# A fused attention and two-layer kernel: q of chunks 1 to 3 scaled into tiles of their own and ahead of the scores, the state products reordered, the first loads in another order, two of three filler groups gone

## The chip, the cores and the metric

The kernel runs on one core of a Trainium2 chip. The metric is the device time of one execution in microseconds (us). Three runs of the kernel before took 582.59, 583.01 and 583.29 us, median 583.01.

## The reference

Linear attention with a decay per head, and then two dense layers with their own activations (B=2, H=8, S=768, D=64; 1536 tokens, d_model 512, d_ff 2048):

```
for t in range(S):                        # attention, state is 64x64 per batch and head
    state = gamma * state + outer(k[t], v[t])
    y[t]  = (1/sqrt(D)) * q[t] @ state
x = y as tokens x 512
h = x @ w_in;  g = max(h,0) + alpha*min(h,0);          x = g @ w_out      # layer 1
h = x @ w2_in; P = a0 + a1 h + a2 h^2 + a3 h^3
Q = 1 + |b0||h| + |b1| h^2;  g = P / (Q + 1e-6);       out = g @ w2_out   # layer 2
```

## The kernel before, in words

**Attention by chunks.** The tokens of the two batches are cut into 12 chunks of 128 (6 per batch). A chunk c has a scores part and an output part. `att_b(c)` (L132) is the scores part: 16 small matmuls (called sc, L139) of the transposed k tile `t` with the q tile, two DVE multiplications by the decay mask `dm_sb` that give `s` (L143), and for every chunk but a batch's first one the scaled q: four ACT multiplications by a constant per piece (L150) and one multiplication by `dq_sb` (L152, POOL for c < 4, DVE after that). For c < 6 the scaled q takes the place of q itself. `att_k(c)` (L114) scales the k tile in place: one POOL instruction (L123), or eight on ACT (L120) for chunks 4 to 7. `att_c(c)` (L154) is the output part: 16 matmuls of v with s into y (L170), 16 of k with v into the state's increment st (L182), 16 of the old state R with the scaled q, added to y (L193, the state product; not for a batch's first chunk), then the new state (L203 for a first chunk, else R = R + st on DVE, L205), and y split into a high part xh (ACT, L212) and a low part xl (DVE, L213). In the text sc1, y1, st1, ys1, xh1, xl1, R1 are these steps of chunk 1, qs1 its scaled q, k1 its scaled k; "b1" and "c1" are its two parts.

**The dense layers.** Weights arrive as 64-bit words and are decoded to a high and a low fp32r half: abs (ACT, L278), word (three DVE instructions, L284, L288, L292), hi (ACT, L303), lo (DVE, L309). `START` gives each half-matrix its half-step and `dec` the half-steps of its four decoding stages; `half(t)` issues what is due at t. A step h is 12 matmuls (`pe_h`, L334: for each of four k-pieces wh with xh, wh with xl, wl with xh); a step acc is 12 more (`pe_out`, L351). There are 96 of each.

**Order.** Every engine executes its instructions in the order in which the program issues them; the order is written out by hand. First come 8 warm-up matmuls and the first loads, all on SP's queue (L526 to L541), then the list `order` (L549): b0, c0, b1, b2, c1, b3, c2, c3, each followed by a `half`. Ahead of c0, b1 and b2 `keep_warm` puts 3, 2 and 3 fp32 filler matmuls on PE (L547; a trace counts two instructions for each). Then b4, and the main loop over the steps, which starts with the first h, c4, b5, the second h, and so on. Chunks 5 to 11 are placed in the main loop by `stages`. `alloc` hands out 42 SBUF slots in the order in which they came free; a load into a reused slot waits for its last user. `load_next(depth)` keeps up to depth raw weight tiles on their way.

Loads 1 to 28 of SP's queue before: q0, t0, dm, cst, k0, v0, q1, t1, w0, q2, t2, k1, v1, dq, q3, t3, k2, v2, k3, v3, w1, w2, alpha, pa, pb, q4, t4, k4 (q, t, k, v of a chunk and dq 256 KB each; dm and each raw weight tile w 512 KB; the others small).

Of the kernel before, what the change touches and what calls it, by code (L numbers as in the profile page):

```python
# [10 lines left out]
AF = mybir.ActivationFunctionType  # L11
# [3 lines left out]
P = 128  # L15
# [16 lines left out]
def tile_fused(  # L32
# [34 lines left out]
    def drop(t):  # L67
        free.append(slot.pop(id(t))[0])
# [19 lines left out]
    def xs(hl, b, ks, sl):  # L88
        return (xh, xl)[hl][b][:, ks, sl]
# [11 lines left out]
    def load_kq(c):  # L101
        nc.sync.dma_start(out=att[c]["q"], in_=qT[c])
        nc.sync.dma_start(out=att[c]["t"], in_=kT[c])  # L103

    def load_nv(c):
        nc.sync.dma_start(out=att[c]["k"], in_=kn[c])
        nc.sync.dma_start(out=att[c]["v"], in_=vn[c])

    def att_load(c):
        att_tiles(c)  # L110
# [15 lines left out]
    def rows(c, j):  # L126
        if c < CPB or j < 2:
            return [(slice(0, P), slice(0, P))]
        h = [slice(0, 64), slice(64, P)]
        return [(h[1], h[0]), (h[0], h[1])]  # L130

    def att_b(c, bank):  # L132
        a = att[c]
        ps = [bank(f"sc{c}_{e}") for e in range(2)]
        for j in range(NK):
            js = slice(j * P, (j + 1) * P)
            for e in range(2):
                es = slice(64 * e, 64 * e + 64)
                nc.tensor.matmul(ps[e][:, js], a["t"][es, js], a["q"][es, js], start=True, stop=True)  # L139
        a["s"] = alloc(f"s{c}")  # L140
        for e in range(2):
            es = slice(512 * e, 512 * e + 512)
            nc.vector.tensor_tensor(out=a["s"][:, es], in0=ps[e], in1=dm_sb[:, es], op=ALU.mult)  # L143
        if c % CPB > 0:
            a["qs"] = a["t"] if c > CPB else a["q"]
            for j in range(NK):
                js = slice(j * P, (j + 1) * P)
                o = 8 * CPB + 4 * (c % CPB) + j
                for ds, es in rows(c, j):
                    nc.scalar.mul(a["qs"][ds, js], a["q"][es, js], cst_sb[es, o:o + 1])  # L150
            eng = nc.gpsimd if c < 4 else nc.vector
            eng.tensor_tensor(out=a["qs"], in0=a["qs"], in1=dq_sb, op=ALU.mult)  # L152

    def att_c(c, ybank, pbank):  # L154
        a = att.pop(c)
        first = c % CPB == 0
        last = c % CPB == CPB - 1
        four = c >= CPB
        ys = [ybank(f"y{c}_{n}") for n in range(1 + four)]


        def yo(j, e):
            js = slice(P * (j % 2), P * (j % 2) + P) if four else slice(j * P, (j + 1) * P)
            return ys[j // 2 if four else 0][64 * e:64 * e + 64, js]

        heads = [(j, e) for j in ((0, 2, 1, 3) if four else range(NK)) for e in range(2)]
        starts = (0, 2) if four else (0,)
        for j, e in heads:
            h = 2 * j + e
            nc.tensor.matmul(  # L170
                yo(j, e),
                a["v"][:, 64 * h:64 * h + 64],
                a["s"][:, 512 * e + j * P:512 * e + (j + 1) * P],
                start=j in starts,
                stop=first and j == NK - 1,
            )
        if not last:
            pst = ys[0][:, 256:512] if four else pbank(f"st{c}")[:, 0:256]
            for j, g in heads:
                e = 1 - g if four and j >= 2 else g  # L180
                hs = slice(64 * (2 * j + e), 64 * (2 * j + e) + 64)
                nc.tensor.matmul(  # L182
                    pst[64 * g:64 * g + 64, 64 * j:64 * j + 64],
                    a["k"][:, hs],
                    a["v"][:, hs],
                    start=not four,
                    stop=not four or (first and j == NK - 1),
                )
        if not first:
            for j, e in heads:  # L190
                g = 1 - e if four and j >= 2 else e
                gs = slice(64 * g, 64 * g + 64)
                nc.tensor.matmul(  # L193
                    yo(j, e),
                    R[gs, j, :],
                    a["qs"][gs, j * P:(j + 1) * P],
                    start=False,
                    stop=j == NK - 1 or (four and j == 1),
                )
        if not last:  # L200
            src = pst.rearrange("p (j d) -> p j d", j=NK)
            if first:
                nc.scalar.copy(R, src)  # L203
            else:
                nc.vector.tensor_tensor(out=R, in0=R, in1=src, op=ALU.add)  # L205
        b, o = divmod(c * P, TB)
        osl = slice(o, o + P)
        for n, y in enumerate(ys):
            js = slice(2 * n, 2 * n + 2) if four else slice(0, 4)
            y2 = y[:, 0:256].rearrange("p (j f) -> p j f", j=2) if four else r4(y)  # L210
            hap = xs(0, b, js, osl)
            nc.scalar.copy(hap, y2)  # L212
            nc.vector.tensor_tensor(  # L213
                out=xs(1, b, js, osl), in0=y2, in1=hap.bitcast(F32), op=ALU.subtract
            )
        for nm in ("qk", "kv", "s"):
            drop(a[nm])


    raw = {}  # L220
# [24 lines left out]
    START = {}  # L245
    for m in A:
        START[0, m, 0], START[0, m, 1] = 2 * m - 9, 2 * m - 4
    START[0, 0, 0] = -10
    for j, m in enumerate(B):
        START[0, m, 0], START[0, m, 1] = 6 + (17 * j) // 5, 8 + (17 * j) // 5  # L250
    for m in range(NF):
# [12 lines left out]
    def load_next(depth):  # L264
        while loaded[0] < len(SEQ) and loaded[0] - loaded[1] < depth:
            k = loaded[0]
            loaded[0] += 1
            l, m, n = SEQ[k]
            r = alloc(f"r{k}", U32)
            nc.sync.dma_start(out=r, in_=SRC[l][n][m].bitcast(U32))  # L270
            words = r.rearrange("p (f t) -> p f t", t=2)
            raw[k] = (words[:, :, 0], words[:, :, 1], r)
# [53 lines left out]
    def pe_h(i):  # L326
        l, b, m, _, _ = STEPS[i]
        wh, wl = W[l, m, 0]
        ps = ring.tile([P, 512], F32, tag="ring", name=f"h{i}")
        n = 0  # L330
        for k in range(NK):
            ks = slice(k * P, (k + 1) * P)
            for w, hl in ((wh, 0), (wh, 1), (wl, 0)):
                nc.tensor.matmul(ps, w[:, ks], xs(hl, b, k, ALL), start=(n == 0), stop=(n == 11))  # L334
                n += 1
        H[i] = ps

    def pe_out(i):
# [143 lines left out]
    N1 = NB * NF  # L482
    dec = {}
    for k, e in enumerate(SEQ):
        for o, nm in zip((0, 1, 2, 3) if k != 1 else (0, 2, 3, 3), ("abs", "word", "hi", "lo")):
            dec.setdefault(START[e] + o, []).append((nm, k))

    NPRE = 12
# [1 line left out]
    def half(t, scalar_last=None, between=None):  # L490
        evs = dec.get(t, ())

        def each(nm):
            return [e[1] for e in evs if e[0] == nm]

        for e in each("abs"):
            w_abs(e)
        for e in each("hi"):
            w_hi(e)
        if scalar_last:  # L500
            scalar_last()
        for e in each("word"):
            w_word(e, 0)
        for e in each("lo"):
            w_lo(e)
        for e in each("word"):
            w_word(e, 1)
        if between:
            between()
        for e in each("word"):  # L510
            w_word(e, 2)
        if later and t % 2 == 0:
            split_x(*later.pop(0))
        load_next(3 if t < -6 else 4 if t < 2 * N1 else 2)

    with tc.manual_schedule():
        wt = alloc("wz")
# [3 lines left out]
        for _ in range(NWARM):  # L521
            nc.tensor.matmul(ps[:, 0:P], wz, wz, start=True, stop=True)
        nc.scalar.preload_act_table_set("natural_log_exp_and_others")
        for c in range(4):
            att_tiles(c)
        load_kq(0)  # L526
        nc.sync.dma_start(out=dm_sb, in_=dm)
        nc.sync.dma_start(out=cst_sb, in_=cst)
        load_nv(0)
        load_kq(1)  # L530
        load_next(1)
        load_kq(2)
        load_nv(1)
        nc.sync.dma_start(out=dq_sb, in_=dq)
        load_kq(3)
        load_nv(2)
        load_nv(3)
        load_next(3)
        nc.sync.dma_start(out=alpha_sb, in_=alpha)
        nc.sync.dma_start(out=ab_sb[:, 0:4], in_=pa.partition_broadcast(P))  # L540
        nc.sync.dma_start(out=ab_sb[:, 4:6], in_=pb.partition_broadcast(P))  # L541
# [6 lines left out]

        order = [("b", 0), ("c", 0), ("b", 1), ("b", 2), ("c", 1), ("b", 3), ("c", 2), ("c", 3)]  # L549
        for n, (s, c) in enumerate(order):  # L550
            if n in (1, 2, 3):
                keep_warm((3, 2, 3)[n - 1])
            if s == "b":
                att_k(c)
                att_b(c, rbank)
            else:
                att_c(c, abank(c % 2), abank(2 + c % 2))
                if c < 2:
                    att_load(4 + c)
            if n == 6:  # L560
                nc.scalar.activation(bb_sb[:, 0:2], ab_sb[:, 4:6], AF.Abs)
                nc.scalar.mul(nalpha_sb, alpha_sb, -1.0)
            half(n - NPRE)
        drop(wt)
        att_b(4, rbank)
        att_k(4)
# [135 lines left out]
```

## Time and profile before

| | before |
|---|---|
| median of three runs | 583.01 us |
| the profiled execution | 584.3 us |
| its span in the profile | 582.5 us |
| mean granted TensorE clock | 0.997 |
| PE busy | 574.3 us, 99% |
| DVE / ACT / POOL busy | 466.2 / 371.1 / 77.5 us |
| HBM read | 47.10 MB |

How to read it: PE is TensorE's matmuls, PEld its weight loads, DVE, ACT and POOL the vector, scalar and GpSimd engines, SP the engine whose queue issues the DMAs. Busy time is the union of an engine's instructions; a matmul's recorded duration overlaps the next one, so the pace of a block of matmuls is read from the start of one block to the start of the next. Times in rows are counted from the span's start.

### The profile page before, as it was taken

Reading aid. Unit: us, or ns where it says so; the run is one execution under the profiler, and the core shown is the slowest. Engines: PE = TensorE matmul, PEld = TensorE weight load, DVE = VectorE, ACT = ScalarE, POOL = GpSimd, SP = SyncE. Lnnn points to the kernel's source line nnn. Section 1 sums busy time; section 2 is a strip of 40 time slices with the busy share of each in tenths; the row PEclk is TensorE's granted clock in tenths of the full one; section 3 lists DMA queues with packets and bytes.
Section 4 is the critical chain, followed back from the end, with each engine's and each line's share of the span. In section 5 each row is a group of like instructions: output and inputs, shape, how many; then the busy total and the mean of one; then the engine's idle time right before and its main releaser. Section 6 shows DMA issues by size and latency. Waiting matters only on the chain.

```text
span 582.5 us, 8124 instructions
## 1 busy us (share of the span) xinstructions
PE 574.3 (99%) x3040; PEld 473.3 (81%) x3040; DVE 466.2 (80%) x738; ACT 371.1 (64%) x679; POOL 77.5 (13%) x61
## 2 busy tenths in 40 slices
PE   8999999999999999999999999999999999999997
PEld 7878777888888888888888888888888888888885
DVE  1899688788684364548997999999998999887886
ACT  2687567656553453437765787777786786686672
POOL 1401100000000000000000312223222222221221
PEclk8999999999999999999999999999999999999999
DMA  8999422334321012112451011001111100010101
GB/s 298 335 379 378 160 73 73 112 106 145 108 73 36 1 37 73 37 37 96 171 203 37 1 37 36 19 19 37 37 37 37 37 0 1 0 73 2 53 19 74
DMA packets 18920, 50.78 MB, mean 87 GB/s; under 512 B 2624, under 2 KB 2752, under 8 KB 18880
## 3 DMA queue, kind: packets, MB, share of 16 engines
q1 hardware_dynamic: 18880, 50.26, 24.8%
q8 instruction: 24, 0.39, 0.3%
q14 instruction: 16, 0.13, 0.1%
HBM read 47.10 MB, written 3.15 MB: 86 GB/s over the span
## 4 chain that ended last, share of the span: by engine, by line
PE 87%; DMA 8%; DVE 2%; SPq 1%; ACT 1%; issue 0%
PE acc L351 43%; PE h L334 42%; DMA qk<-in_qT_dram 2%; DMA r<-in_w1i_dram 1%; DMA r<-in_w1o_dram 1%; DMA kv<-in_vn_dram 1%; DMA dq_sb<-in_dq_dram 1%; DMA kv<-in_kn_dram 1%; ACT qk L150 1%; PE y L170 1%; PE sc L139 1%; DVE p L448 0%; PE y L193 0%; SPq L103 0%; PE y L182 0%
## 5 line engine op out<-in xcount | busy, mean ns | idle before, releaser
L334 PE MATMUL h<-xh,wh 128*128 128x512 f32 x384 | 150.3, 391 | 0.0
L334 PE MATMUL h<-xl,wh 128*128 128x512 f32 x384 | 149.6, 389 | 0.0
L334 PE MATMUL h<-xh,wl 128*128 128x512 f32 x384 | 149.4, 389 | 0.0
L351 PE MATMUL acc<-wh,g 128*128 128x512 f32 x384 | 125.7, 390 | 0.0
L433 POOL TENSOR_TENSOR g<-as,g 128x512 fp32r<-128x512 f32 x47 | 64.6, 1374 | 446.9 <-PE acc L351 261.3
L351 PE MATMUL acc<-g,wh 128*128 128x512 f32 x384 | 118.9, 391 | 0.0
L334 PEld LDWEIGHTS h<-xh,wh 128*128 128x128 f32 x384 | 72.1, 188 | 15.7 <-issue 0.2
L351 PEld LDWEIGHTS acc<-wh,g 128*128 128x128 f32 x384 | 72.0, 188 | 15.6 <-DVE g L433 0.4
L334 PEld LDWEIGHTS h<-xl,wh 128*128 128x128 f32 x384 | 72.1, 188 | 15.0 <-DVE xl L213 0.2
L334 PEld LDWEIGHTS h<-xh,wl 128*128 128x128 f32 x384 | 72.0, 188 | 14.9
L351 PEld LDWEIGHTS acc<-g,wh 128*128 128x128 f32 x384 | 71.6, 188 | 15.5 <-issue 0.7
L303 ACT CAST wh<-z 128x512 fp32r<-128x512 f32 x64 | 39.6, 620 | 57.3 <-DVE z L292 57.3
L351 PE MATMUL acc<-g,wl 128*128 128x512 f32 x192 | 75.0, 391 | 0.7 <-DVE wl L309 0.6
L351 PE MATMUL acc<-wl,g 128*128 128x512 f32 x192 | 74.7, 389 | 0.0
L375 DVE SCALAR_TENSOR_TENSOR np<-np,nalpha_sb 128x512 f32<-128x512 f32 x48 | 36.0, 749 | 40.3 <-ACT np L370 40.3
L369 ACT ACTIVATE np<-h 128x512 f32<-128x512 f32 x48 | 28.5, 595 | 44.2 <-PE h L334 44.2
L396 ACT ACTIVATE as<-h 128x512 f32<-128x512 f32 x48 | 28.6, 596 | 41.3 <-PE h L334 41.3
L402 DVE SCALAR_TENSOR_TENSOR as<-as,bb_sb,rr 128x512 f32<-128x512 f32 x48 | 38.0, 791 | 13.1 <-ACT rr L397 13.1
L385 DVE TENSOR_TENSOR g<-np,g 128x512 fp32r<-128x512 f32 x48 | 33.2, 692 | 17.4 <-ACT g L380 17.2
L292 DVE SCALAR_TENSOR_TENSOR z<-r,z 128x512 uint32<-128x512 uint32 x64 | 44.9, 702 | 1.5
L288 DVE SCALAR_TENSOR_TENSOR z<-r,z 128x512 uint32<-128x512 uint32 x64 | 45.0, 702 | 1.0
L309 DVE TENSOR_TENSOR wl<-z,wh 128x512 fp32r<-128x512 f32 x64 | 45.0, 703 | 0.1
(59 smaller groups left out, 752.0 us busy)
## 6 DMA issues: line engine op xcount, KB each, us to landing
r<-in_w1i_dram SPq DMA_DIRECT2D x16, 512.0 KB, 5.9
r<-in_w1o_dram SPq DMA_DIRECT2D x16, 512.0 KB, 4.2
r<-in_w2i_dram SPq DMA_DIRECT2D x16, 512.0 KB, 3.5
r<-in_w2o_dram SPq DMA_DIRECT2D x16, 512.0 KB, 3.3
qk<-in_qT_dram SPq DMA_DIRECT2D x12, 256.0 KB, 6.1
qk<-in_kT_dram SPq DMA_DIRECT2D x12, 256.0 KB, 6.1
kv<-in_kn_dram SPq DMA_DIRECT2D x12, 256.0 KB, 5.9
kv<-in_vn_dram SPq DMA_DIRECT2D x12, 256.0 KB, 6.0
```

Of the source, the lines that this page charges most:

```text
L288: nc.vector.scalar_tensor_tensor(out=zu, in0=lo, scalar=29, in1=zu, op0=ALU.logical_shift_right, op1=ALU.bitwise_or)
L292: nc.vector.scalar_tensor_tensor(out=zu, in0=hi, scalar=0x80000000, in1=zu, op0=ALU.bitwise_and, op1=ALU.bitwise_or)
L303: nc.scalar.copy(hi, Z[k])
L309: nc.vector.tensor_tensor(out=lo, in0=Z[k], in1=hi.bitcast(F32), op=ALU.subtract)
L334: nc.tensor.matmul(ps, w[:, ks], xs(hl, b, k, ALL), start=(n == 0), stop=(n == 11))
L351: nc.tensor.matmul(acc[0][k], a, c, start=(begin and n == 0), stop=(end != "" and n == 2))
L369: nc.scalar.activation(n, h, AF.Relu, scale=-1.0)
L375: nc.vector.scalar_tensor_tensor(out=p, in0=n, scalar=nalpha_sb[:, m:m + 1], in1=p, op0=ALU.mult, op1=ALU.add)
L385: nc.vector.tensor_tensor(out=gl, in0=p, in1=gh.bitcast(F32), op=ALU.subtract)
L396: nc.scalar.activation(s, h, AF.Square)
L402: nc.vector.scalar_tensor_tensor(out=s, in0=s, scalar=bb_sb[:, 1:2], in1=r, op0=ALU.mult, op1=ALU.add)
L433: eng.tensor_tensor(out=gl, in0=a, in1=gh.bitcast(F32), op=ALU.subtract)
```

## The change

- Scaled q of chunks 1 to 3 goes to a tile of its own (`qt`), and a function `att_q` issues it: for chunk c+1 within the turn of b(c), so qs1, qs2, qs3 are issued in the turns of b0, b1, b2. For c >= 4 it stays inside `att_b` and in place.
- `att_k` moves: k0 after b0 (ahead of qs1), k1 in the turn of b2 (behind qs3), k2 and k3 in that of b3.
- In chunks 0 to 5 the state product ys comes ahead of st on PE, and the state's sum R comes after xh and xl. Chunks 6 to 11 keep their order.
- The filler groups ahead of b1 and b2 go; the one ahead of c0 stays.
- Loads: v ahead of k in each chunk; the new order is q0, t0, dm, cst, v0, k0, q1, t1, dq, q2, t2, w0, v1, k1, q3, t3, v2, k2, v3, k3, w1, q4, t4, w2, v4, k4, w3, alpha, pa, pb. Chunk 4's tiles are taken with the first four, its loads no longer come from c0's turn. The two small ACT instructions that read alpha and pb (L561, L562) go from the turn of c2 to behind c3's.
- `load_next` turns from depth 3 to 4 two half-steps earlier. Weight half 0 has its stages at (0,0,2,2) half-steps in place of (0,1,2,3), weight half 1 at (0,1,2,3) in place of (0,2,3,3); the START of (0,1,0) is the -7 that it was.
- The first h step takes its eight matmuls with xh first, then the four with xl.

```diff
@@ load_nv @@
+        nc.sync.dma_start(out=att[c]["v"], in_=vn[c])
         nc.sync.dma_start(out=att[c]["k"], in_=kn[c])
-        nc.sync.dma_start(out=att[c]["v"], in_=vn[c])
@@ new, in place of the same lines at the end of att_b @@
+    def att_q(c):
+        if c % CPB == 0:
+            return
+        a = att[c]
+        a["qs"] = a["t"] if c > CPB else a["q"]
+        if c < 4:
+            a["qt"] = alloc(f"qs{c}")
+            a["qs"] = a["qt"][:, 0:512]
+        for j in range(NK):
+            js = slice(j * P, (j + 1) * P)
+            o = 8 * CPB + 4 * (c % CPB) + j
+            for ds, es in rows(c, j):
+                nc.scalar.mul(a["qs"][ds, js], a["q"][es, js], cst_sb[es, o:o + 1])
+        eng = nc.gpsimd if c < 4 else nc.vector
+        eng.tensor_tensor(out=a["qs"], in0=a["qs"], in1=dq_sb, op=ALU.mult)
...
+        if c >= 4:
+            att_q(c)
@@ att_c @@
-        if not last:
+        def st_part():
             pst = ys[0][:, 256:512] if four else pbank(f"st{c}")[:, 0:256]
...
+            return pst
+        if four and not last:
+            pst = st_part()
         if not first:
...
+        if not four and not last:
+            pst = st_part()
+        def state_sum():
+            if not last:
...
+        if four:
+            state_sum()
...
+        if not four:
+            state_sum()
@@ pe_h @@
+        prs = [(k, w, hl) for k in range(NK) for w, hl in ((wh, 0), (wh, 1), (wl, 0))]
+        if i == 0:
+            prs.sort(key=lambda e: e[2])
@@ dec, half @@
-        for o, nm in zip((0, 1, 2, 3) if k != 1 else (0, 2, 3, 3), ("abs", "word", "hi", "lo")):
+        for o, nm in zip((0, 1, 2, 3) if k else (0, 0, 2, 2), ("abs", "word", "hi", "lo")):
-        load_next(3 if t < -6 else 4 if t < 2 * N1 else 2)
+        load_next(3 if t < -8 else 4 if t < 2 * N1 else 2)
@@ the loop over order @@
-            if n in (1, 2, 3):
-                keep_warm((3, 2, 3)[n - 1])
+            if n == 1:
+                keep_warm(3)
             if s == "b":
-                att_k(c)
                 att_b(c, rbank)
+                if c == 0:
+                    att_k(0)
+                if c < 3:
+                    att_q(c + 1)
+                for k in ((), (), (1,), (2, 3))[c]:
+                    att_k(k)
             else:
                 att_c(c, abank(c % 2), abank(2 + c % 2))
-                if c < 2:
-                    att_load(4 + c)
-            if n == 6:
-                nc.scalar.activation(bb_sb[:, 0:2], ab_sb[:, 4:6], AF.Abs)
-                nc.scalar.mul(nalpha_sb, alpha_sb, -1.0)
+                if c == 1:
+                    att_load(5)
             half(n - NPRE)
+        nc.scalar.activation(bb_sb[:, 0:2], ab_sb[:, 4:6], AF.Abs)
+        nc.scalar.mul(nalpha_sb, alpha_sb, -1.0)
```

## Rows read from the trace of the kernel before

**Rows 1.** The page: PE's busy line, then DVE and granted clock in 40 slices.
```profile
PE 574.3 (99%) x3040; PEld 473.3 (81%) x3040; DVE 466.2 (80%) x738; ACT 371.1 (64%) x679; POOL 77.5 (13%) x61
...
DVE  1899688788684364548997999999998999887886
```

**Rows 2.** Waits up to 75 us: waiter, line, releaser; total us, times, longest.
```profile
PE y L170 <- DMA kv<-in_vn_dram: 1.8, 1, 1.8
PE acc L351 <- DVE wl L309: 0.6, 1, 0.6
...
PEld h L334 <- DVE xl L213: 0.2, 1, 0.2
```

**Rows 3.** Timeline of PE, 9 to 26 us: start, us, engine, line, operation, names, shapes, count.
```profile
9.23 1.64 PE L170 MATMUL y<-s,kv 128*64 128x128 f32 x16 [1.77 <-DMA kv<-in_vn_dram]
10.60 1.13 PE L182 MATMUL st<-kv 128*64 128x64 f32 x16
11.65 1.22 PE L547 MATMUL warm<-wz 128*128 128x128 f32 x4
...
15.96 1.09 PE L170 MATMUL y<-s,kv 128*64 128x128 f32 x16
16.88 0.64 PE L182 MATMUL st<-kv 128*64 128x64 f32 x16
17.44 1.09 PE L193 MATMUL y<-qk,R 64*64 64x128 f32 x16
18.46 1.16 PE L139 MATMUL sc<-qk 64*128 64x128 f32 x16
19.56 1.09 PE L170 MATMUL y<-s,kv 128*64 128x128 f32 x16
...
24.79 1.16 PE L139 MATMUL sc<-qk 64*128 64x128 f32 x16
25.89 0.50 PE L334 MATMUL h<-xh,wh 128*128 128x512 f32 x1
```

**Rows 4.** Timeline of SP's queue: the issues of v1 and of q3.
```profile
8.52 0.45 SPq L107 DMA_DIRECT2D kv<-in_vn_dram  x1
...
9.78 0.33 SPq L102 DMA_DIRECT2D qk<-in_qT_dram  x1
```

**Rows 5.** DMA issues of these two alone: KB each, us from issue to landing.
```profile
kv<-in_vn_dram SPq DMA_DIRECT2D x1, 256.0 KB, 5.9
...
qk<-in_qT_dram SPq DMA_DIRECT2D x1, 256.0 KB, 6.0
```

**Rows 6.** Timeline of POOL: scaled k1, qs1, k2, qs2.
```profile
13.83 1.04 POOL L123 TENSOR_TENSOR kv<-kv,cst_sb 128x512 f32<-128x512 f32 x1 [4.21 <-DMA dq_sb<-in_dq_dram]
15.24 1.28 POOL L152 TENSOR_TENSOR qk<-qk,dq_sb 128x512 f32<-128x512 f32 x1 [0.37 <-issue]
18.05 1.25 POOL L123 TENSOR_TENSOR kv<-kv,cst_sb 128x512 f32<-128x512 f32 x1 [1.53 <-DMA kv<-in_kn_dram]
19.27 1.73 POOL L152 TENSOR_TENSOR qk<-qk,dq_sb 128x512 f32<-128x512 f32 x1
```

**Rows 7.** Timeline of ACT: the four pieces of qs1, and xh4.
```profile
13.45 1.28 ACT L150 ACTIVATE qk<-qk,cst_sb 128x128 f32<-128x128 f32 x4 [0.83 <-PE sc L139]
...
31.88 0.59 ACT L212 CAST xh<-y 128x512 fp32r<-128x512 f32 x1 [1.64 <-PE y L193]
```

**Rows 8.** PE in quarter-us windows: window, length, busy (instructions), granted clock, DMA share, GB/s.
```profile
9.75:10.00 0.25, 0.25 (x6) 0.50 0.96 393
...
12.75:13.00 0.25, 0.25 (x3) 0.50 1.05 393
```

**Rows 9.** Timeline of DVE: R2, and s5, the instruction behind xl4.
```profile
22.50 0.41 DVE L205 TENSOR_TENSOR R<-R,st 128x256 f32<-128x256 f32 x1
...
33.15 1.28 DVE L143 TENSOR_TENSOR s<-sc,dm_sb 128x512 f32<-128x512 f32 x2
```

**Rows 10.** DMA issues by line: count, KB each, median us to landing.
```profile
ab_sb<-in_pb_dram SPq DMA_DIRECT2D x1, 1.0 KB, 5.2
```

More of the change, by code (lines that the diff above doesn't have):

```diff
@@ L143, in att_b @@
             nc.vector.tensor_tensor(out=a["s"][:, es], in0=ps[e], in1=dm_sb[:, es], op=ALU.mult)
[L144 to L152, printed above, removed]
+        if c >= 4:
+            att_q(c)
     def att_c(c, ybank, pbank):
@@ L199, in att_c @@
                 )
[L200 to L205, printed above, removed]
+        if not four and not last:
+            pst = st_part()
+        def state_sum():
+            if not last:
+                src = pst.rearrange("p (j d) -> p j d", j=NK)
+                if first:
+                    nc.scalar.copy(R, src)
+                else:
+                    nc.vector.tensor_tensor(out=R, in0=R, in1=src, op=ALU.add)
+        if four:
+            state_sum()
         b, o = divmod(c * P, TB)
@@ L215, in att_c @@
             )
-        for nm in ("qk", "kv", "s"):
-            drop(a[nm])
+        if not four:
+            state_sum()
+        for nm in ("qk", "kv", "s", "qt"):
+            if nm in a:
+                drop(a[nm])
     raw = {}
@@ L247, in tile_fused @@
         START[0, m, 0], START[0, m, 1] = 2 * m - 9, 2 * m - 4
-    START[0, 0, 0] = -10
+    START[0, 0, 0], START[0, 1, 0] = -10, -7
     for j, m in enumerate(B):
@@ L329, in pe_h @@
         ps = ring.tile([P, 512], F32, tag="ring", name=f"h{i}")
-        n = 0
-        for k in range(NK):
+        prs = [(k, w, hl) for k in range(NK) for w, hl in ((wh, 0), (wh, 1), (wl, 0))]
+        if i == 0:
+            prs.sort(key=lambda e: e[2])
+        for n, (k, w, hl) in enumerate(prs):
             ks = slice(k * P, (k + 1) * P)
-            for w, hl in ((wh, 0), (wh, 1), (wl, 0)):
-                nc.tensor.matmul(ps, w[:, ks], xs(hl, b, k, ALL), start=(n == 0), stop=(n == 11))
-                n += 1
+            nc.tensor.matmul(ps, w[:, ks], xs(hl, b, k, ALL), start=(n == 0), stop=(n == 11))
         H[i] = ps
@@ L523, in tile_fused @@
         nc.scalar.preload_act_table_set("natural_log_exp_and_others")
-        for c in range(4):
+        for c in range(5):
             att_tiles(c)
@@ L530, in tile_fused @@
         load_kq(1)
+        nc.sync.dma_start(out=dq_sb, in_=dq)
+        load_kq(2)
         load_next(1)
-        load_kq(2)
         load_nv(1)
-        nc.sync.dma_start(out=dq_sb, in_=dq)
         load_kq(3)
@@ L537, in tile_fused @@
         load_nv(3)
+        load_next(2)
+        load_kq(4)
         load_next(3)
+        load_nv(4)
+        load_next(4)
         nc.sync.dma_start(out=alpha_sb, in_=alpha)
```

## The prediction

> **What bounds the kernel now.** I read the page first: PE is busy for 99% of the span, and DVE, at 80% overall, is at nine tenths in the slices from 29 to 58 us [rows 1]. Then PE's waits: up to 75 us there are few, the longest one of 1.8 us for v0, and one of 0.6 us for a low weight half from DVE, which falls at 42 us [rows 2]. So from v0's arrival on the kernel is one stream on PE, and what the change can do is start the first h step earlier or later than 25.89 us [rows 3]; all PE work behind that stays as it was. The reader is to see in PE's timeline that blocks follow each other without a gap from 9.23 us, fillers among them: y takes 0.92 us from start to start (15.96 to 16.88), st 0.56, ys 1.02, sc 1.10 [rows 3]. Last, the timelines of SP, POOL and ACT show what these blocks would wait for if they came earlier or in another order.
>
> **The change, part by part.** Times are those of the one profiled execution, 584.3 us with a span of 582.5; that is 1.3 us above the median of 583.01, and I put the shift found in it onto the median.
>
> Fillers. The group ahead of b1 has 1.22 us [rows 3], the one ahead of b2 six instructions to its four, so at most 1.8 us: 0 to 3.0 us leave PE's stream. None of it reaches the end by itself. c1 needs v1, issued at 8.52 and landed 5.9 us later, at 14.42 [rows 4, 5]. The new list has the same bytes ahead of v1 (dq for k1, both 256 KB), so v1 lands at the same time; c1 starts at about 14.5 in place of 15.96 [rows 3].
>
> Scaled k of chunk 1. Here I see the cost. k1 is now issued on POOL behind qs3, and qs3 needs q3. The same 14 loads stand ahead of q3 in both orders, so it lands as before, 9.78 + 6.0 = 15.78 us [rows 4, 5]. Then four ACT pieces of 1.28 us together [rows 7], then POOL's multiplication, 1.28 or 1.73, then k1, 1.04 or 1.25 [rows 6], and some 0.1 us of handovers. The short pair gives 19.5 us, the long one 20.15. I take 19.5: in the short rows POOL ran beside the mask multiplications, and that is what DVE has to do at 17 to 19 us.
>
> On that choice: 1.28 and 1.73 us are the same instruction, the second beside DVE instructions that read two SBUF tiles [rows 6]. The Trainium skill, page "SBUF — State Buffer", section "Who interferes with whom", says that a DVE instruction with two SBUF inputs contends with a GpSimd instruction that reads SBUF, and one with a single SBUF input does not. By it the mask multiplication, which reads PSUM and one SBUF tile, leaves qs3 at the short price and the stall ends at 19.5; without the rule it could as well be 20.15, and the sum 0.65 us more.
>
> What waits for k1 is st1. c1 runs y1 from 14.5 and ys1 behind it, to 14.5 + 0.92 + 1.02 = 16.44. Then PE waits to 19.5, 3.1 us, and in order behind st1 stand b3, c2, c3, b4 and the first h. b3 starts at 19.5 + 0.56 = 20.06, where it was 18.46 [rows 3]: +1.6.
>
> State product ahead of st, sum behind xl. The sum R2 now comes behind xh2 and xl2. From the start of an xh to the end of its xl it takes 1.27 us (31.88 to 33.15) [rows 7, 9], R 0.41 [rows 9], with handovers about 1.75 after ys2; PE has st2 and y3 to do meanwhile, 0.56 + 0.92 = 1.48. So ys3 waits 0.27. From b3 to b4 that is 1.10 + (0.92 + 1.02 + 0.56) + (0.92 + 0.27 + 1.02 + 0.56) = 6.37 us, against 24.79 - 18.46 = 6.33 before [rows 3]. The first h comes 1.6 to 1.7 us late.
>
> Clock. PE's idle 1.77 us ahead of y0 [rows 3] was followed by a granted clock of 0.50, the level of 1.2 GHz, from 9.75 to 13.0 us [rows 8]. In it y0 took 1.37 us to the next block for 0.92, and st0 1.05 for 0.56 [rows 3]: 0.94 lost in 2.42 us, so about 1.3 in such a stretch. The new idle of 3.1 us is longer than the one that brought this, so I take one more such stretch behind it; it covers the 0.27 of R2. First h: +1.65 + 1.3 - 0.27, about +2.7. Bounds: no drop at all (0), or one twice as long (2.6).
>
> On that idle, the Trainium skill, page "TensorE: Matmul & The Clock Gate", section "What's actually happening", says that "the default state is throttled, and activity releases the throttle". By it the stretch at 0.50 comes back and the sum is +2.3 below; were the clock kept, it would be +1.3.
>
> What is given back behind it. The first h waited 0.2 us for xl3 [rows 2]; with the xh matmuls first it does not. In c4, st goes behind ys, so y4 is complete 0.56 us sooner against PE, while R4 (0.35 at the pace of its neighbours) stands behind xl4. DVE, at nine tenths there [rows 1], is therefore late by 0.2 + 0.56 - 0.35, about 0.4 less than the first h is; PE's 0.6 us wait for DVE at 42 us [rows 2] shrinks by the rest. Net, PE is late by 2.7 - 0.4 = 2.3 us from there to the end. This term lies between 0 and 0.6.
>
> The rest at nothing. v0 ahead of k0: y0 starts a little sooner, but c1's date is v1's. qs1 and qs2 in tiles of their own are the old instructions, issued a chunk sooner: q1 and dq stand at least five transfers ahead of v1, so at 0.68 us each (worked out below) they are down by 11.0, and with 1.28 each on ACT and POOL [rows 6, 7] qs1 is done by 13.6, ahead of ys1 at 15.4; qs2 by 17, ahead of ys2 past 21. What the copies add is three slots of 42. q3's ACT pieces stand ahead of xh1, which loses 0.6 us; R1, behind it, is needed only by ys2, past 21 us. The decode shifts move three DVE instructions ahead of xl3, and the first h needs xl3 only in its last four matmuls. Without that cover the word would cost its 1.8 us of DVE. alpha and pb go behind six transfers of 256 KB: pb landed at about 23.2 with 5.2 us in the queue [rows 10], v1 and q3 with dq and k1 between show 0.68 us for one [rows 4, 5], so 27.3. ACT's two small instructions block qs4's pieces until then; with b4 at 27.5 and later, in place on a q that its scores still read, these wait anyhow. If c1 did not stall, this would cost about 1 us.
>
> **The rivals.**
> B, stall without the slower clock: PE's clock stays at 2.4 GHz. For it: 42 us has a 0.6 us wait with no drop. Against: 1.77 us of idle sufficed [rows 3, 8]. +1.7 - 0.4 = +1.3: 584.3.
> C, not slower: k1 is not late, because q3's pieces and qs3 are done by 15.3, so that k1 ends ahead of 16.44. Then v1 alone is the gate: c1 ends at 17.0, b3 at 18.1, c2 at 20.6, c3 at 23.4, b4 at 24.5, the first h 1.4 us early; if t3 comes only at 18.46, where b3 ran unheld before, nothing is won. pb's wait takes up to 1 us of it, DVE's order gives 0.4. Between 0 and -1.8, middle -0.9: 582.1. It decides at a landing of q3 by 12.7 us, which is 3.1 us sooner than the rows give; that is against it, and nothing in the trace is for it but that a queue's landing may move with the new order.
> D, worse: POOL at the long prices (+0.65) and the clock down for twice as long (+1.3): +4.3, 587.3. For it: a stall of 3.1 us is nearly twice as long as the one seen.
>
> **How the numbers follow.** Forecast 0.55, B 0.20, C 0.13, D 0.12. A measurement can tell 0.2% here, 1.17 us. Forecast and D are slower; B, at +1.3, is slower in six cases of ten; C is faster in a third of its cases. Slower 0.77, same 0.17, faster 0.06. The time is 583.0 + 2.3 = 585.3. The range takes in B and most of D and leaves C out: 583.8 to 587.0.
>
> **What would show it.** In the trace after: one long wait of PE, st (L182's block of chunk 1) for POOL's k, 2.5 to 4 us, ending at 19 to 20.5; POOL in the order k0, qs1, qs2, qs3, k1; q3 landing at 15.5 to 16; a stretch at 0.50 behind the wait; the first h at 27.5 to 29.5. I am wrong if st1 does not wait for POOL, if the first h starts ahead of 26, or if it is late and the end is not.

## The result and the profile after

The changed kernel takes 586.0 us (median of 14 runs, 584.2 to 588.1), the kernel before 582.57 (14 runs, 581.8 to 583.3): a ratio of 1.006 with an interval of 1.005 to 1.007. It is 3.4 us slower. Forecast were +2.3 and 585.3; the time lies in the range.

The profiled execution of the changed kernel has a span of 585.9 us and is one of its longer ones (587.68). Its PE waits up to 75 us, in the columns of [rows 2]:

```profile
PE st L192 <- POOL kv L123: 3.0, 2, 2.8
...
PE y L179 <- DMA kv<-in_vn_dram: 0.8, 1, 0.8
...
PE sc L155 <- DMA qk<-in_kT_dram: 0.7, 1, 0.7
PE acc L374 <- DVE wl L332: 0.4, 1, 0.4
PE y L207 <- DVE R L222: 0.3, 1, 0.3
```

The first line is new: st waits for the k that POOL scales, 2.8 us in one piece. PE's timeline shows which one and what stands behind it, to be read against [rows 3]:

```profile
13.54 1.09 PE L179 MATMUL y<-s,kv 128*64 128x128 f32 x16 [0.80 <-DMA kv<-in_vn_dram]
14.57 1.09 PE L207 MATMUL y<-qs,R 64*64 64x128 f32 x16
18.48 1.12 PE L192 MATMUL st<-kv 128*64 128x64 f32 x16 [2.82 <-POOL kv L123]
19.53 2.08 PE L155 MATMUL sc<-qk 64*128 64x128 f32 x16
21.54 1.97 PE L179 MATMUL y<-s,kv 128*64 128x128 f32 x16
23.45 1.71 PE L207 MATMUL y<-qs,R 64*64 64x128 f32 x16
...
26.99 1.09 PE L207 MATMUL y<-qs,R 64*64 64x128 f32 x16 [0.34 <-DVE R L222]
28.01 0.69 PE L192 MATMUL st<-kv 128*64 128x64 f32 x16
28.62 1.16 PE L155 MATMUL sc<-qk 64*128 64x128 f32 x16
29.72 0.50 PE L358 MATMUL h<-xh,wh 128*128 128x512 f32 x1
```

It is st1, behind y1 and ys1. The scores of b3 take 2.01 us from start to start, against 1.10 in [rows 3], and y2 takes 1.91, against 1.02 in the same order at the full clock (e2 below): the clock is at its lower level. PE in one-us windows (window, length, busy, granted clock, DMA share, GB/s):

```profile
17.00:18.00 1.00, 0.00 (x0) 0.97 1.00 389
18.00:19.00 1.00, 0.52 (x10) 0.50 1.01 391
...
24.00:25.00 1.00, 1.00 (x14) 0.62 1.08 389
```

POOL's timeline answers to [rows 6]: qs3, and behind it k1, k2 and k3 in one group of 3.04 us, so about 1.0 us each.

```profile
16.15 1.27 POOL L146 TENSOR_TENSOR qs<-qs,dq_sb 128x512 f32<-128x512 f32 x1 [2.73 <-ACT qs L144]
17.38 3.04 POOL L123 TENSOR_TENSOR kv<-kv,cst_sb 128x512 f32<-128x512 f32 x3
```

Of the signs that the prediction named, the long wait of st1 (2.8 us), POOL's order and the stretch at 0.50 behind the wait are there. Three dates fall outside their spans: the wait ends at 18.48 (forecast 19 to 20.5), q3 lands at 14.8 (15.5 to 16), and the first h starts at 29.72 (27.5 to 29.5).

### The profile page after: what moved, and what is told of

The parts are those of the page before. It is cut to its first block, busy times and chain, and to the rows that moved or that the text cites. A ratio compares the mean times of both kernels' runs of the same rounds, so it can differ in the third digit from the quotient of the medians.

```text
span 585.9 us, 8101 instructions
## 1 busy us (share of the span) xinstructions
PE 574.0 (98%) x3030; PEld 472.2 (81%) x3030; DVE 465.9 (80%) x738; ACT 371.0 (63%) x679; POOL 76.0 (13%) x61
## 4 chain that ended last, share of the span: by engine, by line
PE 90%; DVE 4%; ACT 2%; DMA 2%; issue 1%; SPq 0%; POOL 0%; DVEq 0%
PE acc L374 43%; PE h L358 42%; DMA qk<-in_qT_dram 2%; PE sc L155 1%; PE y L179 1%; PE y L207 1%; ACT qk L144 1%; DVE z L311 1%; DVE wl L332 1%; DVE np L398 1%; DVE p L471 0%; PE st L192 0%; DVE z L307 0%; ACT kv L120 0%; DVE xl L233 0%
## 5 line engine op out<-in xcount | busy, mean ns | idle before, releaser
L374 PEld LDWEIGHTS acc<-wh,g 128*128 128x128 f32 x384 | 72.0, 188 | 15.5 <-DVE g L456 0.4
L374 PEld LDWEIGHTS acc<-g,wh 128*128 128x128 f32 x384 | 71.6, 188 | 15.5 <-issue 0.7
L358 PEld LDWEIGHTS h<-xl,wh 128*128 128x128 f32 x384 | 72.1, 188 | 14.8
L301 ACT ACTIVATE z<-r 128x512 f32<-128x512 f32 x64 | 42.9, 670 | 3.8 <-DMA r<-in_w1i_dram 3.7
```

The lines of the kernel that those rows point to most:

```text
L301: nc.scalar.activation(z, raw[k][1].bitcast(F32), AF.Abs, scale=2.0**-112)
L374: nc.tensor.matmul(acc[0][k], a, c, start=(begin and n == 0), stop=(end != "" and n == 2))
```

## The experiments

Eleven runs in three groups; the kernel before, timed beside each group, had medians of 582.58, 582.75 and 582.63 us.

**e1: k1 ahead of qs3.**

```
-                for k in ((), (), (1,), (2, 3))[c]:
+                for k in ((), (1,), (), (2, 3))[c]:
```

> The changed kernel with one edit: k1 is scaled on POOL in the turn of b1, ahead of qs3, in place of behind it. Theory (the loss is st1's wait for k1 and the slower clock behind it): k1 lands at about 14.1 us and is done by 15.2, st1 does not wait for POOL, no stretch at 0.50 behind it, first h at 23.5 to 25.0 us, time 0.5 to 1.8 us below the kernel before. Rival 1 (the other load order, the missing fillers or the new order of state product and sum cost it): the time stays 1.5 to 3.5 us above the kernel before although the wait is gone.

583.34 us, ratio 1.0016 (1.0007 to 1.0024): 2.7 us below the changed kernel, but not below the kernel before. The wait is gone and the clock stays at 1.00, so the wait and its clock were most of the loss, and rival 1 is left with 0.8 us. The gain that I expected behind them did not come: the first h starts at 25.56, not by 25.0. The trace names what took it. PE, then ACT:

```profile
16.04 0.69 PE L192 MATMUL st<-kv 128*64 128x64 f32 x16
...
22.84 1.09 PE L207 MATMUL y<-qs,R 64*64 64x128 f32 x16 [1.08 <-DVE R L222]
```

```profile
20.49 0.67 ACT L301 ACTIVATE z<-r 128x512 f32<-128x512 f32 x1 [2.99 <-DMA r<-in_w1i_dram]
21.07 0.57 ACT L232 CAST xh<-y 128x512 fp32r<-128x512 f32 x1
...
27.23 0.20 ACT L593 ACTIVATE bb_sb<-ab_sb 128x2 f32<-128x2 f32 x1 [1.60 <-DMA ab_sb<-in_pb_dram]
27.34 0.20 ACT L594 ACTIVATE nalpha_sb<-alpha_sb 128x16 f32<-128x16 f32 x1
27.45 1.26 ACT L144 ACTIVATE qk<-qk,cst_sb 128x128 f32<-128x128 f32 x4
```

st1 follows ys1 at once, but ys3 waits 1.08 us for R2, which is behind xl2, xh2 and, on ACT, the abs of a weight that lands at 20.5. A second hold follows: ACT waits 1.6 us for pb, with qs4 behind it.

**e2: PE kept at work during the wait.** In the changed kernel, between ys1 and st1:

```
+        if c == 1:
+            w = abank(3)("warm1")
+            for _ in range(9):
+                nc.tensor.matmul(w[:, 0:P], wz, wz, start=True, stop=True)
```

> The changed kernel with nine filler matmuls (18 recorded instructions, about 2.6 us at the full clock) put on PE between ys1 and st1, so that PE works while k1 is late. Theory (two costs, the wait and the slower clock): st1 still starts when POOL is done, within 0.3 us of before the edit, the granted clock stays at 1.00 behind it, the time is 1.0 to 2.0 us above the kernel before, some 1.5 to 2.5 below the changed kernel. Rival 2 (the wait alone makes the whole loss, the clock costs nothing): 3.0 to 3.8 us above the kernel before, as the changed kernel.

584.73 us (584.35 to 584.96), ratio 1.0037 (1.0025 to 1.0049): 1.3 us below the changed kernel's median, a little less than expected, and 2.2 above the kernel before, a little more. The gap between ys1 and st1 is as long as in the changed kernel (16.10 to 18.99, 2.89 us), with fillers in it, and the clock stays up:

```profile
16.10 2.27 PE L217 MATMUL warm<-wz 128*128 128x128 f32 x18
18.99 0.69 PE L192 MATMUL st<-kv 128*64 128x64 f32 x16 [0.61 <-POOL kv L123]
19.60 1.16 PE L155 MATMUL sc<-qk 64*128 64x128 f32 x16
20.70 1.09 PE L179 MATMUL y<-s,kv 128*64 128x128 f32 x16
21.72 1.09 PE L207 MATMUL y<-qs,R 64*64 64x128 f32 x16
...
26.27 1.16 PE L155 MATMUL sc<-qk 64*128 64x128 f32 x16
27.37 0.50 PE L362 MATMUL h<-xh,wh 128*128 128x512 f32 x1
```

```profile
19.00:20.00 1.00, 1.00 (x22) 1.00 1.08 414
```

So the clock is a cost of its own, 1.3 us at the median. Most of the scatter goes with it: of the 14 runs of the changed kernel, the four with a mean granted clock of 0.998 or more took 584.2 to 585.3 us, the three at 0.993 587.7 to 588.1, while e2's five lie within 0.6 us. It is not all of the scatter: one run at 0.997 took 587.7.

**e3: a late k1 in the kernel before.**

```
-                att_k(c)
+                for k in ((0,), (), (2, 1), (3,))[c]:
+                    att_k(k)
```

> The kernel before with one edit: k1 is scaled on POOL behind k2 (done at 19.3 us) in place of ahead of qs1; nothing else of the change. Theory (a late k1 is enough): POOL ends k1 at about 20.3, st1 waits some 3.4 us, a stretch at 0.50 follows, the time is 3 to 5.5 us above the kernel before. Rival 1 (the loss needs the other edits): within 1 us of the kernel before.

588.18 us, ratio 1.0101 (1.0088 to 1.0114), +5.6 us, the expected direction and just past the upper end. One instruction moved on POOL is enough; a stretch at 0.50 follows here too, from 19.25 to 22.6 us:

```profile
PE st L182 <- POOL kv L123: 4.2, 1, 4.2
```

**e4: the fillers back, k1 late.**

```
-            if n == 1:
-                keep_warm(3)
+            if n in (1, 2, 3):
+                keep_warm((3, 2, 3)[n - 1])
```

> The changed kernel with the two filler groups ahead of b1 and b2 put back, k1 still late. Theory (the fillers only fill waits for t2 and v1, which hold PE anyway): 2.8 to 4.0 us above the kernel before, as the changed kernel within 0.6. Rival 3 (taking the fillers away is what lets the clock fall): 1 us or more below the changed kernel, with no or a shorter stretch at 0.50.

585.07 us (583.4 to 586.1), ratio 1.0038 (1.0024 to 1.0053), 0.9 below the changed kernel: between the two expectations. PE's waits for t2 and v1 are gone and c1 starts at 13.52 as without fillers, so they do fit into those waits. The stretch at 0.50 in the one trace (19.9 to 23.2 us) is about half as long as the changed kernel's. The intervals of the two kernels still touch at 1.005, and I leave open whether the fillers save clock here.

**e5, e6, e7: the two further holds.** On top of e1: e5 puts the state's sum ahead of xh and xl again, e6 puts the ACT instructions that read alpha and pb behind b4 and k4, e7 does both.

```
-        if four:
-            state_sum()
+        state_sum()
...
-        if not four:
-            state_sum()
```

```
-        nc.scalar.activation(bb_sb[:, 0:2], ab_sb[:, 4:6], AF.Abs)
-        nc.scalar.mul(nalpha_sb, alpha_sb, -1.0)
...
         att_b(4, rbank)
         att_k(4)
+        nc.scalar.activation(bb_sb[:, 0:2], ab_sb[:, 4:6], AF.Abs)
+        nc.scalar.mul(nalpha_sb, alpha_sb, -1.0)
```

> e1_k1_ahead_of_qs3 with one edit more: the state's sum R of chunks 1 to 5 again ahead of xh and xl, the products still in the new order. In e1's trace ys3 waits 1.1 us for R2, which stands behind xl2 and xh2, and xh2 behind the abs of a weight that lands at 20.5 us; behind b4, ACT waits to 27.2 us for pb and DVE 1.8 us for qs4. Theory (two holds in a row, R2 and then pb): the wait for R2 goes, the first h starts about 1.0 us sooner, ys4 then waits about 1 us for qs4, and the time stays within 0.4 us of e1. Rival (R2's place is all that is left): 0.8 to 1.1 us below e1.

> e1_k1_ahead_of_qs3 with one edit more: the two small ACT instructions that read alpha and pb stand behind b4 and k4, so qs4 no longer waits for pb; R's sum stays late. Theory: qs4 is done about 1.6 us sooner, xl4 about 0.4, PE's wait for the weight half at 42 us shrinks by as much: 0.2 to 0.6 us below e1. Rival (constants later cost nothing): within 0.2 us of e1.

> e1 with both edits, of e5 and of e6. Theory: the two holds are in a row, so only both give the sum: 1.2 to 1.7 us below e1, 0.3 to 1.0 below the kernel before. Rival (DVE's own work sets the pace behind 26 us): no more than 0.5 us below e1.

e5 took 582.82 us (ratio 1.0006, 0.9997 to 1.0014), e6 583.35 (1.001, 1.0001 to 1.0019), e7 581.71 (0.998, 0.997 to 0.9991). Against e1 the single edits bring 0.5, which is not clear of the noise (its interval and e1's overlap), and nothing; both together bring 1.6. So e7's theory holds: the two holds stand in a row. For e6 its rival came, since the pb edit alone is worth nothing. In e5's trace the R2 wait is replaced by one for qs4:

```profile
28.59 1.09 PE L207 MATMUL y<-qk,R 64*64 64x128 f32 x16 [0.59 <-DVE qk L146]
```

In e6's it is still there, 1.82 us long in that trace. e7 has neither wait and is 1.0 us faster than the kernel before.

**e8: the kernel before once more**, for a second trace.

> The kernel before, unchanged, for a second trace of it: in the first one dm landed at 7.6 us, in every trace of the changed kernel and of its variants at 6.1 to 7.1. If that is a difference of executions and not of kernels, dm lands here at 6.2 to 7.2, v1 near 13.5, and the first h starts at 24.0 to 25.5 where the first trace had 25.89; if it belongs to the kernel, 7.4 or later and 25.9.

Its one run took 582.58 us, with a span of 580.8. PE's timeline:

```profile
8.63 1.09 PE L170 MATMUL y<-s,kv 128*64 128x128 f32 x16 [2.13 <-DMA kv<-in_vn_dram]
9.53 0.66 PE L182 MATMUL st<-kv 128*64 128x64 f32 x16
...
13.96 1.09 PE L170 MATMUL y<-s,kv 128*64 128x128 f32 x16
...
16.96 1.16 PE L139 MATMUL sc<-qk 64*128 64x128 f32 x16
...
24.87 0.50 PE L334 MATMUL h<-xh,wh 128*128 128x512 f32 x1
```

c1 starts at 13.96 and the first h at 24.87, where [rows 3] have 15.96 and 25.89. The stretch at 0.50 of [rows 8] does not occur in this execution, and dm landed at 6.5 us in place of 7.6. The trace from which I predicted was a slow start of this kernel. e3's trace bears this out: up to c1 it is the kernel before on PE, and its c1 starts at 13.84.

This trace also corrects what the prediction set against rival B, that 1.77 us of idle sufficed for the drop. Here PE waits 2.13 us ahead of y0, and the granted clock stays at 1.00; y0 takes 0.90 us to the next block, where it took 1.37 in [rows 3]. The length of a wait alone does not decide whether the clock falls.

**e9: e7 with the late k1**, its `att_k` line as the change has it.

> e7_both with k1 put back behind qs3: the late k1 alone, on the version without the other two holds. Theory: the wait (e2 over e1: 1.4 us) and the slower clock behind it (changed kernel over e2: 1.3 us) come back whole: 2.2 to 3.4 us above e7, which is 1.2 to 2.4 above the kernel before. Rival (the holds at R2 and pb hide behind a late k1, so that they are free there): the changed kernel's 586.0 comes back, 3.6 us or more above e7.

586.33 us, ratio 1.0057 (1.0042 to 1.0072): 4.6 us above e7 and level with the changed kernel. My theory of a sum falls, the rival holds: with a late k1 it makes no difference that can be told from the noise whether R2 and pb are repaired. e9's trace has the same 2.8 us for st1 as the changed kernel's. It puts b3 at 19.35 where e7's has 16.00 (e9 first, then e7):

```profile
13.81 1.09 PE L179 MATMUL y<-s,kv 128*64 128x128 f32 x16 [0.81 <-DMA kv<-in_vn_dram]
...
18.73 0.69 PE L192 MATMUL st<-kv 128*64 128x64 f32 x16 [2.81 <-POOL kv L123]
19.35 1.99 PE L155 MATMUL sc<-qk 64*128 64x128 f32 x16
```

```profile
13.34 1.09 PE L179 MATMUL y<-s,kv 128*64 128x128 f32 x16 [0.82 <-DMA kv<-in_vn_dram]
...
16.00 1.16 PE L155 MATMUL sc<-qk 64*128 64x128 f32 x16
```

Of these 3.35 us, 0.47 is the later start of c1 in that execution and 2.88 the wait. With e2's 1.3 for the clock the wait makes 4.2 of the measured 4.6; what the other 0.4 is stays open.

**e10: v1 and k1 ahead of the first weight tile**, on top of e7, with the word stage of weight half 0 one half-step later.

```
-        for o, nm in zip((0, 1, 2, 3) if k else (0, 0, 2, 2), ("abs", "word", "hi", "lo")):
+        for o, nm in zip((0, 1, 2, 3), ("abs", "word", "hi", "lo")):
...
+        load_nv(1)
         load_next(1)
-        load_nv(1)
```

> e7_both with v1 and k1 loaded ahead of the first weight tile w0 (512 KB) and the word stage of weight half 0 one half-step later, behind s2. In e7's trace PE waits 0.8 us for v1. Theory (v1's landing is the next gate): v1 lands 1.3 us sooner, the wait for v1 goes, the first h starts 0.6 to 0.9 us sooner, the time is 0.2 to 0.9 us below e7. Rival (DVE's order or the weight, now late, takes it back): within 0.2 us of e7 or above it.

581.04 us (580.5 to 583.0), ratio 0.9977 (0.9966 to 0.9987). PE's wait for v1 is gone from the trace, but the first h starts only 0.3 us sooner than e7's (23.48 for 23.77), less than expected. The median is 0.7 below e7's, as expected, but the intervals of the two overlap. It beats both kernels.

**e11: e7 with the two filler groups back.**

> e7_both with the two filler groups ahead of b1 and b2 put back. Theory (they only fill waits for t2 and v1, and e7's clock stays at 1.00 without them): within 0.4 us of e7. Rival (the missing fillers cost clock in part of the executions, as e4's 0.9 us under the changed kernel could mean): 0.5 us or more below e7.

582.4 us, ratio 0.9995 (0.9986 to 1.0004), 0.7 above e7: outside my expectation, and on the other side from the rival. Once k1 is on time, taking the fillers away is worth 0.7 us by the medians, but the two intervals overlap, so this gain is not shown.

## Why the prediction was right, and by how much it was off

**The cause.** "k1 is now issued on POOL behind qs3, and qs3 needs q3" holds: the wait is in the trace of the changed kernel, goes with e1, and comes in the kernel before by e3. POOL took the short pair, 1.27 and 1.0 us: qs3 beside the end of a mask multiplication and beside xl1, k1 with DVE idle; in e1, where qs3 ran beside the mask multiplications, it took 1.28. The rule of the Trainium skill, page "SBUF — State Buffer", section "Who interferes with whom", by which a DVE instruction with at most one SBUF input, outside the 2-port perf modes, does not contend with GpSimd, agrees with the 1.27 and the 1.28. Predicted were a wait of 3.1 us that ends at 19.5; it is 2.82 and ends at 18.48, since q3 landed at 14.8 and not at 15.78; v1 too came a microsecond sooner than in the trace of before, at 13.4 for 14.42.

**The term that was mis-sized** is "b3 starts at 19.5 + 0.56 = 20.06, where it was 18.46 [rows 3]: +1.6". Against e8's trace b3 goes from 16.96 to 19.53, +2.6. I credited the change with starting c1 at 14.5 in place of 15.96, a gain of 1.46; it is 13.54 for 13.96, 0.4. The rest of that gain was not the change's: the trace of before held a stretch at 0.50 and late loads, which e8's does not. In e8 v1 lands at 13.9 and c1 starts at once, so there the fillers hold nothing up and v1 is the gate in both orders. I had shifted the result onto the median by the profile's 1.3 us, but had not asked what in that execution made it 1.3 us long. That missing 1.0 us is the larger part of 3.4 - 2.3. The medians say the same without any one trace: e2, with the wait and without the lower clock, is 2.2 above the kernel before, where the forecast for that case (rival B) was 1.3; the clock adds 1.3, where it had 1.0 net.

**Two smaller readings.** From b3 to b4 the forecast had 6.37 us; e2's trace has 6.67 (19.60 to 26.27), because y with ys behind it takes 1.02 and not 0.92. And of the two transfers behind the 0.68 us, only dq stands between v1 and q3 in the old order, not k1; the number is not changed by it.

**The clock.** Predicted were +1.3 for a stretch, 1.0 of it net; e2 measures 1.3 at the median. It does not come every time: one of the 14 runs had a mean granted clock of 1.000 (584.8 us). In the profiled execution the stretch is twice as long (18 to 24.7 us, against 9.75 to 13.0), which was the larger half of rival D; the other, POOL's long prices, did not come, so that this execution's 587.7 us lie near D's 587.3 by chance. The Trainium skill's sentence in "TensorE: Matmul & The Clock Gate", section "What's actually happening", that activity releases the throttle, agrees with e2: with fillers in the same wait the granted clock is 1.00.

**What is given back.** From e8 to e2 the first h moves by 2.5 us (24.87 to 27.37) and the span by 2.1 (580.8 to 582.9): 0.4, as predicted. But from the first h to the end the two traces of the kernel before differ by 0.7 (556.6 and 555.9), so these 0.4 are not shown. PE's wait for DVE in the acc step is 0.4 for 0.6.

**State sum behind xl.** 0.34 us in the trace for 0.27 forecast. What I had not seen is ACT's queue ahead of xh2: there the abs waits for its weight. With k1 late it is done in time; without, ys3 waits 1.1 us (e1).

**Constants later** I costed at nothing behind the stall, and at about 1 us without it. e9 agrees with the first. For the second, e5 shows 0.6 us of PE waiting for qs4, and e7 is 1.1 below e5.

**Rival C** was excluded by the trace, and its size does not stand up either: without the late k1 the changed kernel is e1, 0.8 above the kernel before and not 0.9 below it. My C had the pb wait in it and lacked the wait for R2, and it rested on the same early start against [rows 3].

As the change stands, the 3.4 are 2.7 for the late k1 (the changed kernel over e1) and 0.8 for the rest (e1 over before). With the two further holds repaired, which with a late k1 makes no difference (e9), they are 4.6 for the late k1 (e9 over e7) less 1.0 that the repaired rest gains (e7 below before), within 0.2.

## What to carry to other kernels

When instructions are moved on an in-order engine, look at what each one now stands behind: k1 was put behind a product that had to wait for a later load and for another engine, and the matmul that needed it stopped everything on PE. A second trace of the kernel before is worth its cost before differences of a microsecond are argued from one: the first of these was 1.7 us longer than the second (spans of 582.5 and 580.8). And the largest hold hides the next two: R2 and pb cost nothing that could be measured until k1 was on time, and repairing one of them alone brought no gain clear of the noise.

## What had not been expected of the hardware

A wait of 2.8 us on PE had a second price that varies from run to run: with the same program the mean granted clock was 0.993 in the run of 588.1 us and 0.998 in that of 584.2. Fillers in the wait took the scatter from 3.9 us (14 runs) to 0.6 (5 runs). And a wait does not always bring this price: PE kept a granted clock of 1.00 through 2.13 us of idle ahead of y0 in e8's trace, and lost it after 1.77 us at the same place of the same kernel in the first trace.
